# Attention with a mixture of experts: the softmax reciprocal moved to the product with V, that product issued earlier, one step more of depth, and the first weight split on GpSimd

## The chip, the core and the metric

The kernel runs on one core of a Trainium2 chip. Its engines work through instruction lists of their own, in order: PE (TensorE, matrix products and transposes), DVE (VectorE), ACT (ScalarE), POOL (GpSimd) and SP (SyncE, which here issues DMAs). They meet by semaphores. The metric is the device time of one execution in microseconds (us), the median over runs. Before the change it is 853.65 us (three runs, 851.12 to 854.62).

## What is computed

```python
# 4 batches, 8 heads, 512 local + 32 global tokens, head size 64
out_g = softmax(q_g @ k_all.T / 8) @ v_all                 # global rows see all 544 keys
s_l   = concat([q_l @ k_g.T / 8, where(|i - j| <= 32, q_l @ k_l.T / 8, -1e9)])
out_l = softmax(s_l) @ concat([v_g, v_l])                  # local rows: a window, and the globals
# softmax(s) = exp(s - max) / (sum + 1e-9)
x = tokens of out_g, out_l                                 # 2304 tokens of 512
e = argmax(x @ w_gate);  x = gate * sigmoid(x @ w_output_gate)[e] * (relu(x @ w1[e]) @ w2[e])
h = x @ w_in;  out = (P(h) / (Q(h) + 1e-6)) @ w_out        # P cubic, Q quadratic in |h|
```

## The kernel before

The program has three stages: attention (to about 168 us), eight experts, and the last two products. The change lies in the first, and in the first expert's weights, which are prepared during it.

Attention works through 72 units. A local unit ("l") holds 128 query rows of a pair of heads against a window of 160 keys; there are 64, four to a pair of heads. A global unit ("g") holds the global rows of four heads against all 544 keys; there are 8. Each unit passes through stages, and a loop over steps `s` (line 430) issues at each step one stage of several units, so that units are in flight together:

- `s0`: PE multiplies Q and K into the PSUM tile `sc` (L258; L287 for a global unit). DVE adds the mask and takes the row maximum (L263, one instruction for each of two heads).
- `s1`, one step later: ACT takes the exponential and the row sums (L301).
- `s2`, two steps later: POOL adds the two column blocks of `ex` that stand for the global keys (L312) and adds 1e-9 to the sums (L320, tile `r`, or `rg` for a global unit). Then, behind a `yield`, DVE takes the reciprocal (L322).
- `s3`, `KT` = 4 steps later: PE transposes `ex` (L331), DVE copies it out of PSUM as `pts`, ACT in one unit of four (L333).
- `s4`, `KV` = 5 steps later: PE multiplies by V (L358; L369 for a global unit) into the PSUM tile `xv`. After every second local unit DVE multiplies both by the reciprocals into `xrow` (L361). The next product into `xv` waits for that. For a global unit ACT scales (L373).
- `s5`, `KX` = 7 steps later: PE transposes `xrow` (L399), and ACT copies it (L400).

Within a step the order of issue is the first part of `s2`, `s3`, the reciprocal of `s2`, two background calls, `s0`, a background call, `s1`, another, `s4`, `s5`, a last background call, and then loads. The loop makes 81 steps; the last nine or so only empty the pipeline. `step_bg()` advances background work by one `yield`: the routing of the batch just done (`gate`, a chain of small DVE instructions with some products on PE, L489 to L619), and, after the third batch, `ahead`. This gathers, scales and transposes the first expert's rows in three blocks: "g" is an indirect DMA of POOL (L780), "x" a scaling on DVE (L794), "p" four transposes on PE with their copies (L805, L785, L786). The table `AH` gives the background calls to let pass before each of these nine actions.

From step 25, in one step of four, one of 16 pieces of the first expert's weights is split into a rounded part `hi` and a rest `lo` (`W0`, `split_piece`, mode `SM0` = "act_pool"): ACT casts `hi` (L691), POOL subtracts (L695). What is left goes behind the loop.

Loads are issued by SP three pairs of heads ahead, into four buffers of each kind. After the loop the first expert's product starts (L898), and the routing of the last batch is woven into it.

Of the kernel before, what the change touches and what calls it, by code (L numbers as in the profile page):

```python
# [7 lines left out]
F32 = mybir.dt.float32  # L8
# [5 lines left out]
AF = mybir.ActivationFunctionType  # L14
ALU = mybir.AluOpType
# [13 lines left out]


WN = 15
SLAST, GW, GS, SPL, AH = 1, 3, 2, 8, (0, 0, 14, 1, 2, 0, 2, 24, 2)
NW = 0
XG = lambda nc, h: nc.vector.tensor_copy
OY = 0
# [51 lines left out]
CH = (4, 3, 4, 3, 3)  # L87
ER = {"ab": 1, "q": 2, "u": 2, "r0": 1}
CQ = lambda nc: nc.sync
SM0 = "act_pool"  # L90
KT, KV, KX = 4, 5, 7
LL = 2
OA = lambda nc, i: nc.vector
SB_ = 2
# [8 lines left out]
class Build:  # L103
# [94 lines left out]
    def attention(self, ap):  # L198
        nc, tc, t = self.nc, self.tc, self.t
        with ExitStack() as st:  # L200
# [3 lines left out]
            sp, gp, vp, lp = P("sp", 3), P("gp", 1), P("vp", 2), P("lp", 4)  # L204
# [20 lines left out]
            def load_pair(g):  # L225
                if g < B * NP:
                    load_qk(g)
                    load_v(g)

            def load_b(b):  # L230
                if b >= B:
                    return
                qg[b] = vp.tile([128, NP, 64], F32, tag="qg", name="qg")
                nc.sync.dma_start(out=qg[b], in_=t["qg"][b])
# [8 lines left out]
            st_, rs = {}, {}  # L243
# [50 lines left out]
            def s1(u):  # L294
                k = units[u]
                src, mx = st_[u]
                ssum = sp.tile([128, 2], F32, tag="ssum", name="ssum")
                if k[0] == "l":
                    ex = sp.tile([128, 2, 160], F32, tag="ex", name="ex", bufs=KT)
                    for h in range(2):  # L300
                        nc.scalar.activation(ex[:, h], src[:, h], AF.Exp, bias=mx[:, h:h + 1], scale=-1.0,  # L301
                                             accum_out=ssum[:, h:h + 1])
                else:
                    ex = gp.tile([128, S], F32, tag="exg", name="exg")
                    nc.scalar.activation(ex, src, AF.Exp, bias=mx[:, 0:1], scale=0.125, accum_out=ssum[:, 0:1])
                st_[u] = ex, ssum

            def s2(u):
                k = units[u]
                ex, ssum = st_[u]  # L310
                if k[0] == "l":
                    nc.gpsimd.tensor_tensor(out=ex[:, :, 0:32], in0=ex[:, :, 0:32], in1=ex[:, :, 128:160], op=ALU.add)  # L312
                    if k[3] % 2 == 0:
                        self.r = sp.tile([128, 2, 2], F32, tag="r", name="r")
                    r = self.r[:, k[3] % 2]
                    rs[k[1:3] + (k[3] // 2,)] = self.r
                else:
                    r = rs[u] = sp.tile([128, 1], F32, tag="rg", name="rg", bufs=1)
                    ssum = ssum[:, 0:1]
                nc.gpsimd.tensor_scalar(out=r, in0=ssum, scalar1=1e-9, scalar2=None, op0=ALU.add)  # L320
                yield
                nc.vector.reciprocal(out=r, in_=r)  # L322
                st_[u] = ex

            def s3(u):
                k = units[u]
                pr = st_[u]
                pt = ps_t.tile([128, 4, 128], F32, tag="pt", name="pt")
                if k[0] == "l":
                    for h in range(2):  # L330
                        nc.tensor.transpose(pt[:, h, :], pr[:, h, 0:128], self.ident)  # L331
                    pts = sp.tile([128, 2, 128], F32, tag="pts", name="pts", bufs=KV - KT + 1)
                    (nc.scalar.copy if k[3] in PA else nc.vector.tensor_copy)(pts, pt[:, 0:2])  # L333
                else:
                    pt2 = ps_t.tile([128, 4, 128], F32, tag="pt", name="pt")
                    pts = gp.tile([128, 7, 128], F32, tag="ptg", name="ptg")
                    for c, (at, rows, _) in enumerate(GCH):
                        nc.tensor.transpose((pt, pt2)[c // 4][:rows, c % 4], pr[:, at:at + rows], self.ident)
                    nc.vector.tensor_copy(pts[:, 3], pt[:, 3])
                    nc.vector.tensor_copy(pts[:96, 0:3], pt[:96, 0:3])  # L340
                    nc.scalar.copy(pts[:32, 5:7], pt2[:32, 1:3])
                    nc.scalar.copy(pts[:64, 4], pt2[:64, 0])
                st_[u] = pts

            def s4(u):
                k = units[u]
                pts = st_.pop(u)
                if k[0] == "l":
                    _, b, p, i = k
                    g = b * NP + p  # L350
                    if i % 2 == 0 and p == 0:
                        xrow[b, i // 2] = xp.tile([128, 2, DM], F32, tag="xrow", name="xrow")
                    if i % 2 == 0:
                        self.xv = next(halves)
                    xps = self.xv.rearrange("p (i h d) -> p i h d", i=2, h=2)
                    for h in range(2):
                        for j in range(4):
                            nc.tensor.matmul(xps[32 * j:32 * j + 32, i % 2, h], lhsT=pts[:, h, 32 * j:32 * j + 32],  # L358
                                             rhs=vw[g][:, 4 * i + j, 64 * h:64 * h + 64], start=True, stop=True)
                    if i % 2 == 1:  # L360
                        nc.vector.tensor_tensor(  # L361
                            out=xrow[b, i // 2][:, :, 128 * p:128 * p + 128].rearrange("p i (h d) -> p i h d", h=2), in0=xps,
                            in1=rs.pop((b, p, i // 2)).unsqueeze(3).to_broadcast([128, 2, 2, 64]), op=ALU.mult)
                else:
                    _, b, q = k
                    xps = next(halves)[:, 0:64]
                    for c, (_, rows, n) in enumerate(GCH):
                        for a in range(4):
                            nc.tensor.matmul(xps[32 * a:32 * a + 32], lhsT=pts[:rows, c, 32 * a:32 * a + 32],  # L369
                                             rhs=vw[b * NP + 2 * q + a // 2][:rows, n, 64 * (a % 2):64 * (a % 2) + 64],  # L370
                                             start=(c == 0), stop=(c == len(GCH) - 1))
                    xr = gp.tile([128, 64], F32, tag="xr", name="xr", bufs=2)
                    nc.scalar.activation(xr, xps, AF.Copy, scale=rs.pop(u))  # L373
                    nc.sync.dma_start(
                        out=self.xbuf[S * b:S * b + SG, 256 * q:256 * q + 256].rearrange(
                            "t (a d) -> a t d", a=4), in_=xr)
                    st_[u] = xr
# [44 lines left out]
            n = len(units)  # L422
            w0 = self.split_set(0, SM0)
            when, at = {}, {u[1:]: k for k, u in enumerate(units)}
# [3 lines left out]
                    k = min(k, at[B - 1, 1, 0])  # L428
                when.setdefault(k, []).append(g)
            for s in range(n + KX + LL):  # L430
                norm = s2(s - 2) if 0 <= s - 2 < n else iter(())
                next(norm, None)
                if 0 <= s - KT < n:
                    s3(s - KT)
                next(norm, None)
                for _ in range(NB):
                    self.step_bg()
                if s < n:
                    s0(s)
                self.step_bg()  # L440
                if 0 <= s - 1 < n:
                    s1(s - 1)
                self.step_bg()
                if 0 <= s - KV < n:
                    s4(s - KV)
                if 0 <= s - KX < n:
                    s5(s - KX)
                self.step_bg()
                for g in when.get(s, ()):
                    load_pair(g)  # L450
                    if g % NP == 0:
                        load_b(g // NP)
                if s in RS:
                    self.load_raw(0, RS.index(s))
                while pend and pend[0][0] <= s:
                    i = pend.pop(0)[1]
                    if i == 0:
                        self.lfin = ps_s.tile([128, 2, 512], F32, tag="sc", name="lfin")
                        self.lgs = self.gt.tile([128, 512], F32, tag="lgs", name="lgs", bufs=1)
                    o = self.lfin[:, 0, 256 * i:256 * i + 256]  # L460
                    self.logits(o, xT[B - 1, i])
                    nc.scalar.copy(self.lgs[:, 256 * i:256 * i + 256], o)
                if W0(s):
                    next(w0, None)
# [945 lines left out]
```

## Time and profile before

| | us |
|---|---|
| median of three runs (lowest, highest) | 853.65 (851.12, 854.62) |
| the profiled execution | 850.67 |
| its span, first to last instruction | 849.1 |
| PE, DVE, ACT, POOL busy in the span | 788.6, 602.1, 542.9, 355.0 |
| mean granted TensorE clock | 0.974 |

The rows below come from this one profiled execution, and times in it count from the start of its span. Busy time of PE is the union of its matrix instructions, whose ends are modelled. "PEld" is the loading of weights into PE, which overlaps. "PEclk" is the share of full clock that was granted. In the views of waits, "A <- B" says that an instruction of A was held last by B; "issue" is time in which the engine waited for nothing that the profile shows. A name before `<-` in an instruction is its output, the names behind are inputs.

### The profile page before, as it was taken

What the parts mean: (1) busy time and instruction counts of PE and PEld (TensorE: products, weight loads), DVE (VectorE), ACT (ScalarE), POOL (GpSimd) and SP (SyncE); (2) the same over time, 40 slices, a digit from 0 to 9 for tenths busy, and PEclk for the clock granted to TensorE, in tenths of its full rate; (3) what the DMA queues carried; (4) which work ended last, traced back from release to release, by engine and by line L of the source; (5) the groups of instructions that cost most, each with busy time, mean ns of one, the idle gap of its engine ahead of it and who ended that gap; (6) DMA issues with size and microseconds to landing.
All of it is one profiled execution on the core that took longest, in us unless ns stands there. A gap on an engine that the chain in (4) does not pass through costs nothing. (4 is left out here: it accounts for less than half of the span.)

```text
span 849.1 us, 17307 instructions
## 1 busy us (share of the span) xinstructions
PE 788.6 (93%) x6261; PEld 663.8 (78%) x6262; DVE 602.1 (71%) x1385; ACT 542.9 (64%) x1205; POOL 355.0 (42%) x419
## 2 busy tenths in 40 slices
PE   8998888688799999999997999999999999999995
PEld 4665555487697999999795788888878889888883
DVE  4766577485273987876186999868878886788784
ACT  4765664543463666665256888767777775777774
POOL 2333333445161666563062677542243324233332
PEclk9998999988899999999999999999999999999999
DMA  9796662356273888988144432011010001000100
GB/s 354 238 354 240 247 225 84 93 169 187 72 238 135 263 318 286 331 290 280 53 168 126 132 97 91 1 50 37 14 38 13 13 1 38 13 2 0 38 1 37
DMA packets 50702, 113.91 MB, mean 134 GB/s; under 512 B 8707, under 2 KB 22292, under 8 KB 48554
## 3 DMA queue, kind: packets, MB, share of 16 engines
q1 hardware_dynamic: 41946, 98.23, 34.4%
q0 software_dynamic: 4288, 10.06, 3.5%
q10 hardware_dynamic: 4368, 4.34, 1.5%
q8 instruction: 56, 0.92, 0.4%
q14 instruction: 44, 0.36, 0.2%
HBM read 96.99 MB, written 19.56 MB: 137 GB/s over the span
## 5 line engine op out<-in xcount | busy, mean ns | idle before, releaser
L1185 POOL TENSOR_TENSOR q<-q,ab 128x384 f32<-128x384 f32 (+1 forms) x80 | 101.8, 1273 | 203.1 <-ACT q L1184 194.9
L1221 PE MATMUL acc<-slot,gh 128*128 128x512 f32 x544 | 171.1, 395 | 3.7 <-ACT gh L1193 1.9
L695 POOL TENSOR_TENSOR slot<-raw,slot 128x512 fp32r<-128x512 f32 x80 | 110.0, 1379 | 104.1 <-ACT slot L691 100.7
L1114 PE MATMUL ph<-x2c,slot 128*128 128x512 f32 (+1 forms) x576 | 132.5, 379 | 5.6 <-DVE u L1187 3.9
L1114 PEld LDWEIGHTS ph<-x2c,slot 128*128 128x128 f32 x576 | 106.5, 189 | 26.4 <-DVE u L1187 5.1
L1221 PEld LDWEIGHTS acc<-slot,gh 128*128 128x128 f32 x544 | 101.1, 187 | 25.7 <-ACT gh L1193 2.8
L1221 PE MATMUL acc<-slot,gl 128*128 128x512 f32 x272 | 107.6, 396 | 0.3 <-DVE gl L1194 0.3
L910 PE MATMUL acc<-hT,slot 128*128 128x256 f32 (+1 forms) x768 | 105.2, 288 | 0.2 <-DVE hT L904 0.2
L910 PEld LDWEIGHTS acc<-hT,slot 128*128 128x128 f32 x768 | 98.0, 191 | 0.5 <-DVE hT L904 0.4
L691 ACT CAST slot<-raw 128x512 fp32r<-128x512 f32 x144 | 84.9, 618 | 9.3 <-DVE yt L916 5.9
L1196 ACT ACTIVATE r<-q,cab 128x384 f32<-128x384 f32 (+1 forms) x80 | 52.8, 660 | 45.7 <-POOL q L1185 45.5
L1202 DVE SCALAR_TENSOR_TENSOR q<-q,r 128x384 f32<-128x384 f32 (+1 forms) x64 | 38.0, 593 | 52.0 <-ACT r L1198 51.9
L1114 PE MATMUL ph<-xa,slot 128*128 128x384 f32 x384 | 72.0, 336 | 1.5 <-DVE u L1209 1.5
L1193 ACT CAST gh<-u 128x384 fp32r<-128x384 f32 (+1 forms) x80 | 44.6, 558 | 42.1 <-DVE u L1209 35.2
L1114 PEld LDWEIGHTS ph<-xa,slot 128*128 128x128 f32 x384 | 67.7, 188 | 4.6 <-DVE u L1209 1.9
L695 DVE TENSOR_TENSOR slot<-raw,slot 128x512 fp32r<-128x512 f32 x64 | 60.4, 946 | 13.3 <-ACT slot L691 12.5
L301 ACT ACTIVATE ex<-sm,mx 128x160 f32<-128x160 f32 x128 | 53.6, 421 | 13.1 <-DVE mx L263 11.7
L1221 PEld LDWEIGHTS acc<-slot,gl 128*128 128x128 f32 x272 | 50.9, 187 | 13.4 <-DVE gl L1194 1.0
L1184 ACT ACTIVATE q<-ab,cab 128x384 f32<-128x384 f32 (+1 forms) x80 | 59.8, 747 | 0.0
L1183 ACT ACTIVATE u<-ph,cab 128x384 f32<-128x384 f32 (+1 forms) x80 | 56.7, 709 | 0.0
L1187 DVE SCALAR_TENSOR_TENSOR u<-u,cab,ph 128x384 f32<-128x384 f32 (+1 forms) x80 | 53.4, 668 | 2.8
L898 PE MATMUL ph<-xa,slot 128*128 128x256 f32 x384 | 53.8, 293 | 1.2 <-ACTq L996 1.2
(212 smaller groups left out, 1466.5 us busy)
## 6 DMA issues: line engine op xcount, KB each, us to landing
raw<-in_w_dram SPq DMA_DIRECT2D x76, 512.0 KB, 6.7
vw<-in_vw_dram SPq DMA_DIRECT2D x16, 1024.0 KB, 9.7
r<-in_w_dram SPq DMA_DIRECT2D x20, 512.0 KB, 5.6
kw<-in_kw_dram SPq DMA_DIRECT2D x16, 384.0 KB
raw<-wf SPq DMA_DIRECT2D x10, 512.0 KB, 4.8
xg<-ybuf SPq DMA_DIRECT2D x17, 256.0 KB, 4.4
qt<-in_qT_dram SPq DMA_DIRECT2D x16, 256.0 KB, 4.8
xbuf<-xrow SPq DMA_DIRECT2D x8, 512.0 KB
```

The costliest lines, as they stand in the source:

```text
L301: nc.scalar.activation(ex[:, h], src[:, h], AF.Exp, bias=mx[:, h:h + 1], scale=-1.0, accum_out=ssum[:, h:h + 1])
L691: nc.scalar.copy(hi, r)
L695: eng.tensor_tensor(out=lo[:, c], in0=r[:, c], in1=hi[:, c].bitcast(F32), op=ALU.subtract)
L898: nc.tensor.matmul(ph, lhsT=W[:, b, 2 * k + s // 4, c:c + 128], rhs=x[:, a, k, :n], start=(i == 0), stop=(i == 11))
L910: nc.tensor.matmul(acc[m][:, :n], lhsT=W[:, b, 8 + f, 128 * m:128 * m + 128], rhs=hT[f % nh][:, a, :n], start=(f == 0 and i == 0), stop=(f ...
L1114: self.nc.tensor.matmul(ph[:, :w], lhsT=l[a], rhs=r[b], start=(k == 0 and i == 0), stop=(k == 3 and i == 2))
L1183: nc.scalar.activation(u, h, AF.Identity, scale=a3, bias=a2)
L1184: nc.scalar.activation(q, ab, AF.Identity, scale=b1, bias=b0)
L1185: nc.gpsimd.tensor_tensor(out=q, in0=q, in1=ab, op=ALU.mult)
L1187: nc.vector.scalar_tensor_tensor(out=u, in0=u, scalar=a1, in1=h, op0=ALU.add, op1=ALU.mult)
L1196: nc.scalar.activation(r0, q, AF.Ln, bias=eps1)
L1221: nc.tensor.matmul(accs[i], lhsT=l[a], rhs=Wo[:, b, f, :], start=(f == 0 and j == 0), stop=(f == 15 and j == 2))
```

## The change

- `s2` no longer takes the reciprocal. `s4` does: for a local unit once for two units, on all four sums of a row, just ahead of the second product with V; for a global unit just ahead of ACT's scaling.
- `s4` is issued right behind `s3` and ahead of the scores of `s0`. `KT`, `KV` and `KX` grow by one to 5, 6 and 8, so the loop has 82 steps. `r` gets four buffers, `rg` two.
- `SM0` = "pool": POOL makes `hi` itself with a copy, and then subtracts (`split_piece`, unchanged). ACT has no part in the 16 pieces.
- `AH` changes: the nine delays are 3, 5, 11, 3, 5, 0, 5, 20, 2 calls, before 0, 0, 14, 1, 2, 0, 2, 24, 2.

```diff
-SLAST, GW, GS, SPL, AH = 1, 3, 2, 8, (0, 0, 14, 1, 2, 0, 2, 24, 2)
+SLAST, GW, GS, SPL, AH = 1, 3, 2, 8, (3, 5, 11, 3, 5, 0, 5, 20, 2)
...
-SM0 = "act_pool"
-KT, KV, KX = 4, 5, 7
+SM0 = "pool"
+KT, KV, KX = 5, 6, 8
...
             def s2(u):
...
                     if k[3] % 2 == 0:
-                        self.r = sp.tile([128, 2, 2], F32, tag="r", name="r")
+                        self.r = sp.tile([128, 2, 2], F32, tag="r", name="r", bufs=4)
...
                 nc.gpsimd.tensor_scalar(out=r, in0=ssum, scalar1=1e-9, scalar2=None, op0=ALU.add)
-                yield
-                nc.vector.reciprocal(out=r, in_=r)
                 st_[u] = ex
...
             def s4(u):
...
+                    if i % 2 == 1:
+                        r = rs.pop((b, p, i // 2))
+                        nc.vector.reciprocal(out=r, in_=r)
                     for h in range(2):
                         for j in range(4):
                             nc.tensor.matmul(xps[32 * j:32 * j + 32, i % 2, h], lhsT=pts[:, h, 32 * j:32 * j + 32],
...
-                    nc.scalar.activation(xr, xps, AF.Copy, scale=rs.pop(u))
+                    r = rs.pop(u)
+                    nc.vector.reciprocal(out=r, in_=r)
+                    nc.scalar.activation(xr, xps, AF.Copy, scale=r)
...
             for s in range(n + KX + LL):
-                norm = s2(s - 2) if 0 <= s - 2 < n else iter(())
-                next(norm, None)
+                if 0 <= s - 2 < n:
+                    s2(s - 2)
                 if 0 <= s - KT < n:
                     s3(s - KT)
-                next(norm, None)
+                if 0 <= s - KV < n:
+                    s4(s - KV)
                 for _ in range(NB):
                     self.step_bg()
                 if s < n:
                     s0(s)
...
-                if 0 <= s - KV < n:
-                    s4(s - KV)
```

On DVE, two neighbouring steps early in attention, where no background work stands between, read before (`ISA` is the mask step with its read of the maximum):

```order
L322 RECIPROCAL r<-r 128x2
L263 ISA sm,mx<-sc,mask 128x160
L263 ISA mx 128x1
L263 ISA sm,mx<-sc,mask 128x160
L263 ISA mx 128x1
L333 COPY pts<-pt 128x256
L322 RECIPROCAL r<-r 128x2
L263 ISA sm,mx<-sc,mask 128x160
L263 ISA mx 128x1
L263 ISA sm,mx<-sc,mask 128x160
L263 ISA mx 128x1
L361 TENSOR_TENSOR xrow<-xv,r 128x2x128
```

And with the change (line numbers shift by two or so):

```order
L331 COPY pts<-pt 128x256
L263 ISA sm,mx<-sc,mask 128x160
L263 ISA mx 128x1
L263 ISA sm,mx<-sc,mask 128x160
L263 ISA mx 128x1
L331 COPY pts<-pt 128x256
L356 RECIPROCAL r<-r 128x4
L362 TENSOR_TENSOR xrow<-xv,r 128x2x128
L263 ISA sm,mx<-sc,mask 128x160
L263 ISA mx 128x1
L263 ISA sm,mx<-sc,mask 128x160
L263 ISA mx 128x1
```

One reciprocal for a pair of units stands where two stood, and the multiplication into `xrow` has moved from behind the mask steps of its step to ahead of them.

On POOL, around the first weight piece (`slot_81` is the first expert's weight buffer), the list reads before:

```order
L312 TENSOR_TENSOR ex<-ex 128x2x32
L320 TENSOR_SCALAR r<-ssum 128x2
L695 TENSOR_TENSOR slot_81<-raw_74,slot_81 128x512
L312 TENSOR_TENSOR ex<-ex 128x2x32
L320 TENSOR_SCALAR r<-ssum 128x2
```

And with the change:

```order
L312 TENSOR_TENSOR ex<-ex 128x2x32
L320 TENSOR_SCALAR r<-ssum 128x2
L690 CAST slot_81<-raw_74 128x512
L691 TENSOR_TENSOR slot_81<-raw_74,slot_81 128x512
L312 TENSOR_TENSOR ex<-ex 128x2x32
L320 TENSOR_SCALAR r<-ssum 128x2
```

The cast has come into POOL's list, ahead of the subtraction; the sums of the next unit stand behind both, as they stood behind the one.

On PE, from the last scores but one on (`xg_90`, `xg_91` are gathered rows of the first expert), before:

```order
L331 MATMUL pt<-ident,ex 128x128 x2
L258 MATMUL sc<-kw,qt 64x160 x4
L358 MATMUL xv<-vw,pts 32x64 x8
L385 MATMUL pt<-ident,xr 64x128
L331 MATMUL pt<-ident,ex 128x128 x2
L258 MATMUL sc<-kw,qt 64x160 x4
L805 MATMUL pt<-ident,xg_90 128x128 x4
L358 MATMUL xv<-vw,pts 32x64 x8
L805 MATMUL pt<-ident,xg_91 128x128 x4
L331 MATMUL pt<-ident,ex 128x128 x2
```

And with the change, from the last scores on:

```order
L258 MATMUL sc<-kw,qt 64x160 x4
L388 MATMUL pt<-ident,xr 64x128
L329 MATMUL pt<-ident,ex 128x128 x2
L359 MATMUL xv<-vw,pts 32x64 x8
L329 MATMUL pt<-ident,ex 128x128 x2
L359 MATMUL xv<-vw,pts 32x64 x8
L491 MATMUL pt<-xTg,cst 32x128 x4
L402 MATMUL pt<-ident,xrow 128x128 x2
L329 MATMUL pt<-ident,ex 128x128 x2
L359 MATMUL xv<-vw,pts 32x64 x8
L484 MATMUL pt<-ident,xrow 128x128
L807 MATMUL pt<-ident,xg_90 128x128 x4
```

The transposes of the first gathered block stood right behind the last scores; now three transposes of `ex` and three products with V stand between.

## Rows read from the trace of the kernel before

**Rows 1.** Busy us by stretch: PE, PEld, DVE, ACT, POOL; then PEclk, DMA share, GB/s
```profile
24.00:64.00 40.00, 38.94 (x783) 26.65 (x784) 28.77 (x151) 27.41 (x111) 13.45 (x44) 1.00 0.90 314
...
64.00:144.00 80.00, 66.54 (x1206) 44.57 (x1205) 52.08 (x289) 45.65 (x177) 28.02 (x73) 0.91 0.61 209
...
144.00:168.00 24.00, 16.92 (x310) 10.17 (x307) 12.28 (x55) 12.48 (x45) 10.24 (x18) 0.93 0.23 72
```

**Rows 2.** The same stretches, score products alone (L258): PE, PEld
```profile
24.00:64.00 40.00, 9.93 (x160) 4.03 (x160) 1.00 0.90 314
...
64.00:144.00 80.00, 15.47 (x232) 6.34 (x232) 0.91 0.61 209
```

**Rows 3.** The same view, weight casts on ACT alone (L691)
```profile
64.00:144.00 80.00, 5.52 (x9) 0.91 0.61 209
```

**Rows 4.** Waits of PE, 64 to 144: us in total, times, longest
```profile
PE xv L358 <- DVE xrow L361: 5.6, 7, 1.8
...
PE xv L369 <- DVE xrow L361: 1.4, 2, 1.2
...
PE pt L331 <- DVE r L322: 1.4, 2, 0.7
...
PE pt L331 <- DVE pts L333: 1.1, 1, 1.1
```

**Rows 5.** Waits of DVE, same stretch
```profile
DVE r L322 <- POOL r L320: 12.3, 8, 2.0
```

**Rows 6.** Timeline, one weight piece: start, us, engine, line, shapes, [idle before]
```profile
84.64 0.61 ACT L691 CAST slot<-raw 128x512 fp32r<-128x512 f32 x1
...
85.32 1.27 POOL L695 TENSOR_TENSOR slot<-raw,slot 128x512 fp32r<-128x512 f32 x1 [2.71 <-ACT slot L691]
...
86.66 0.22 POOL L320 TENSOR_SCALAR rg<-ssum 128x1 f32<-128x1 f32 x1
...
86.92 0.16 DVE L322 RECIPROCAL rg<-rg 128x1 f32<-128x1 f32 x1 [1.46 <-POOL rg L320]
...
88.01 0.43 PE L358 MATMUL xv<-vw,pts 128*32 128x64 f32 x16 [1.20 <-DVE xrow L361]
```

**Rows 7.** Groups of PE instructions, 64 to 144, of the gate: busy us, mean ns
```profile
L615 PE MATMUL ta<-ob,oa 128*128 128x136 f16 x11 | 2.2, 252 | 0.0
...
L489 PE MATMUL lgT<-xT,cst 128*32 128x256 f32 x32 | 2.1, 385 | 0.0
...
L514 PE MATMUL lg<-ident,lgs 128*128 128x128 f32 x8 | 1.3, 287 | 0.3 <-ACT lgs L509 0.3
```

**Rows 8.** Timeline, DVE instructions beside long POOL instructions
```profile
138.91 0.31 DVE L604 TENSOR_SCALAR ob<-iota,slf,cst 128x136 f16<-128x136 f16 x1
...
140.84 1.39 DVE L604 TENSOR_SCALAR ob<-iota,slf,cst 128x136 f16<-128x136 f16 x1
...
140.92 1.26 POOL L695 TENSOR_TENSOR slot<-raw,slot 128x512 fp32r<-128x512 f32 x1 [1.37 <-PE sc L258]
...
169.92 2.13 DVE L521 COPY L<-Lg 128x16 f32<-128x16 f32 x1
```

**Rows 9.** Groups of POOL copies, whole span: busy us, mean ns
```profile
L161 POOL CAST tri<-cst 128x256 bf16<-128x256 f32 x1 | 0.4, 393 | 0.0
...
L155 POOL COPY run_cnt<-cst 128x8 f32<-128x8 f32 x1 | 0.2, 194 | 0.1
```

**Rows 10.** Group of DVE mask steps, 8 to 168
```profile
L263 DVE CUSTOM_DVE_ANT_0 sm<-sc,mask 128x160 f32<-128x160 f32 x124 | 34.9, 319 | 5.9 <-PE sc L258 3.8 <-ACT ex L301 0.8 <-PE pt L331 0.3
```

**Rows 11.** Timeline of PE, one undisturbed step
```profile
31.65 0.38 PE L331 MATMUL pt<-ident,ex 128*128 128x128 f32 x2
...
32.39 0.43 PE L358 MATMUL xv<-vw,pts 128*32 128x64 f32 x16
```

**Rows 12.** Timeline behind the last scores
```profile
153.66 0.17 DVE L322 RECIPROCAL r<-r 128x2 f32<-128x2 f32 x1 [2.20 <-POOL r L320]
...
155.66 1.01 PE L805 MATMUL pt<-ident,xg 128*128 128x128 f32 x4 [3.00 <-issue]
```

More of the change, by code (lines that the diff above doesn't have):

```diff
@@ L317, in s2 @@
                 else:
-                    r = rs[u] = sp.tile([128, 1], F32, tag="rg", name="rg", bufs=1)
+                    r = rs[u] = sp.tile([128, 1], F32, tag="rg", name="rg", bufs=2)
                     ssum = ssum[:, 0:1]
                 nc.gpsimd.tensor_scalar(out=r, in0=ssum, scalar1=1e-9, scalar2=None, op0=ALU.add)
-                yield
-                nc.vector.reciprocal(out=r, in_=r)
                 st_[u] = ex
@@ L362, in s4 @@
                             out=xrow[b, i // 2][:, :, 128 * p:128 * p + 128].rearrange("p i (h d) -> p i h d", h=2), in0=xps,
-                            in1=rs.pop((b, p, i // 2)).unsqueeze(3).to_broadcast([128, 2, 2, 64]), op=ALU.mult)
+                            in1=r.unsqueeze(3).to_broadcast([128, 2, 2, 64]), op=ALU.mult)
                 else:
```

## The prediction

> **What bounds the kernel now.** I read the busy time by stretch first, to see where PE, the busiest engine, stands idle. From 24 to 64 us it is busy for 38.94 of 40 us at full clock; from 64 to 144 for 66.54 of 80, at a mean granted clock of 0.91 [rows 1]. The reader is to see a stage in two halves that do the same work at two speeds. Counting that work comes next. A local unit issues eight records of L258, so the first stretch makes 160/8 = 20 local units, 2.0 us each, and the second 232/8 = 29, 2.76 us each [rows 2]. Global units are spread evenly among them. What differs is that the weight pieces have begun: nine casts in the second stretch [rows 3].
>
> Third came the waits. PE's largest are for the multiplication into `xrow` (5.6 and 1.4 us), for the reciprocal (1.4) and for a copy behind it (1.1) [rows 4], all work of DVE. DVE's largest wait in turn is the reciprocal's, for POOL: 12.3 us in eight times [rows 5]; nine pieces, eight long waits. Last I followed one piece through the timeline: ACT casts at 84.64, POOL subtracts from 85.32 to 86.59, so the sum of a unit comes out only at 86.66 to 86.88. The reciprocal has stood 1.46 us at the head of DVE's queue, with the mask steps and `xrow` behind it, and PE has waited 1.20 us for `xrow` when it goes on at 88.01 [rows 6]. So POOL is idle most of the time (28.02 of 80 us busy [rows 1]), and yet its order bounds the stage: a long instruction of POOL stands ahead of a short one on which DVE waits within the same step.
>
> **The reciprocal and the order of issue.** The change takes that wait away: the reciprocal stands four steps behind the sum it reads, 4 x 2.0 = 8 us. POOL's other product, the added columns, is read by PE's transposes three steps later, 6 us, against one piece of some 2 us.
>
> What is it worth? At the pace of the first stretch, the 29 units take 58.0 us; the gate's products, mostly absent there, add 2.2 + 2.1 + 1.3 = 5.6 [rows 7], together 63.6. The ceiling is 80 - 63.6 = 16.4 us, and it holds PE's idle time as well as what the lower clock costs. Of the idle 80 - 66.54 = 13.46 us, the four waits of [rows 4] are 9.5, or 71%; the others belong to other causes and stay. 0.71 x 16.4 = 11.6 us. The clock I take along with the waits, since it stands at 1.00 where PE does not stall and at 0.91 where it does [rows 1]: of its two levels, 1.2 and 2.4 GHz, a mean of 0.91 means 18% of the time at the lower.
>
> There are 32 + 8 reciprocals for 64 + 8, and at 0.16 us [rows 6] DVE saves 32 x 0.16 = 5.1 us. I count nothing: DVE is busy 52.08 of 80 us [rows 1], so the time it saves lies beside PE; 5.1 is the other end.
>
> What is late next? `xrow` now stands ahead of the mask steps and waits for the product, which PE issues right behind the transposes; DVE's copy of `pts` covers nearly all of it. In the eight global units ACT's scaling waits for the product and has two exponentials behind it that stood ahead. Uncovered, that is at most a step each, 8 x 2.0 = 16 us; the exponentials are transposed four steps (8 us) later, so I take nothing. On SP the store of the global rows falls one step behind against the loads, which run three pairs, 12 units or 24 us, ahead: nothing. V's buffers come free later by about one pair of transposes; the same cover.
>
> **The split on POOL.** ACT loses 16 casts of 0.61 us [rows 6]. It is busy 45.65 of 80 [rows 1] and no wait of PE in [rows 4] names it: nothing. POOL gains 16 copies that the trace does not have. From below: 393 ns for 256 columns and 194 for 8 give 0.80 ns a column [rows 9], hence 0.194 + 504 x 0.0008 = 0.60 us. From above: the two-input subtraction of the same tile, 1.27 us [rows 6]. I take 0.60, for a one-input cast is what the nearest row shows; the range keeps 1.27. A piece then holds POOL for 0.60 + 1.27 = 1.87 us (2.54 at most), in about 7.5 us, and the queue behind it has the three steps of cover named above. The Trainium skill, "GPSIMD Engine Reference", section 3.1, gives 769 ns for 512 elements of a one-input loop; by it a piece would be 2.04 us, and the sum the same.
>
> The copies do have a price on DVE. Of the gate's instructions one of L604 took 1.39 us in place of 0.31: it began at 140.84 and ended at 142.23, as POOL's subtraction ended (140.92 + 1.26 = 142.18) [rows 8]. One hit in nine pieces cost 1.1 us. A window longer by 1.87/1.27 is hit more often and holds longer, by 1.47 each, so 1.1 becomes 2.4, 1.3 more. Every piece in full would be 9 x 1.87 = 16.8. I take 2.5, near the row, raised because copy, subtraction and the sums behind them will now run without a gap.
>
> **Depth, delays and the tail.** One step more of depth is one more step to empty: a transposition and a product, 0.38 + 0.43 = 0.8 us [rows 11]. Against it, PE stood 3.00 us at 152.66 before the first gathered block, whose transposes stood right behind the last scores; DVE had come late to its scaling after a reciprocal that waited 2.20 us for POOL [rows 12]. That wait goes, and the block stands three products later. The other end is that the wait moves to the third block, whose gather follows the first block's transposes more closely: up to the same 3.0 back. I take 3.0 - 0.8 = 2.2 gained, and keep -0.8 for the range. The buffers cost nothing. What follows attention (routing of the last batch, gathers, first expert) hangs on its end and shifts with it.
>
> **Sum.** 11.6 - 2.5 + 2.2 = 11.3 us. The profiled span of 849.1 becomes 837.8; with the 850.67 - 849.1 = 1.57 us around it, 839.4. The profiled execution lay 853.65 - 850.67 = 2.98 below the median, so the median to expect is 842.4, say 842. At the good end (whole ceiling, whole gap, no price on DVE: 16.4 + 3.0 - 0.8 = 18.6) it is 835; the forecast's own range is 835 to 848.
>
> **Rivals.**
>
> *Slower: the pieces block DVE.* The mechanism is that of [rows 8], its place the three gates and the tail, its price up to 1.87 us a piece. Before it, the gain is 11.6 + 2.2 = 13.8. Over 16 pieces it decides from 13.8/16 = 0.86 us a piece, and the kernel is slower by more than 0.5% from (13.8 + 4.3)/16 = 1.13. With 13 pieces in full, 24.3 us, the time is 853.65 - 13.8 + 24.3 = 864. For it: a copy of 16 columns took 2.13 us [rows 8]. Against it: the 124 mask steps average 319 ns with a dozen pieces beside them [rows 10], so most of DVE's work is not touched. Chance 7%. The Trainium skill speaks against the change here: "SBUF — State Buffer", section "Who interferes with whom", says that GpSimd and VectorE share a port pair as an exclusive lock, which a VectorE instruction needs if it has two inputs in SBUF or runs in a two-port mode, and that the later one blocks fully. The L604 that ended with POOL's instruction agrees; by the rule alone any such instruction that meets a piece pays in full.
>
> *No change: new waits for the old.* DVE stays in order behind PE, the gates bring its small instructions in bunches, and half of the 11.6 comes back as waits of PE for `pts` and `xrow`; the tail's wait moves to the third block. Then 5.8 - 2.5 - 0.8 = 2.5 us are gained: 851. For it: PE also waits for ACT and for the gate, 13.46 - 9.5 = 4 us that stay. Against it: from 24 to 64 us the same DVE work with the same order leaves PE 1.06 us idle [rows 1]. Chance 15%.
>
> *The gain is given back later.* If the transfers behind attention set the pace of the first experts, half remains: 853.65 - 5.6 = 848. Against it: the DMA share is 0.23 at the end of attention, and inside it 0.61, which at 68 us for 80 becomes 0.72, under the 0.90 that the first stretch bears [rows 1]. Chance 5%.
>
> **Chances.** The forecast has 73%. About 0.5%, 4.3 us, is what a measurement of this kernel can tell from no change. The forecast and the third rival lie beyond it: faster 78%; same 15%; slower 7%. The range of 835 to 851 leaves out the slower rival, half of the second, and the forecast's edges.
>
> **What would show it.** In the profile after: no reciprocal of `r` waits for POOL, where 12.3 us stood. From 64 us to the end of attention, a local unit takes 2.2 to 2.4 us, and the granted clock is above 0.95. POOL's copy takes 0.6 to 0.8 us. `xrow` no longer leads PE's waits. The first expert's product starts some 11 us before 168. I am wrong if L604, L600 and their like average far over their 0.3 us (the first rival), if PE waits as long for `pts` or `xrow` as before (the second), or if attention ends 11 us sooner and the span does not (the third).

## The result, and the profile after

The changed kernel took 845.62 us (median of four runs), the kernel before 854.13 beside it. The ratio is 0.9898 [0.9852, 0.9945]. A repeat in five rounds gave 843.77 (842.38 to 844.53) against 852.72, 0.9897 [0.9865, 0.9929]: some 8.8 us faster. One of the first four executions, the profiled one, took 1492.84 us for a reason that no run here shows; the ratio leaves it out, and the profile shown here is of the repeat.

First the busy time by stretch of the profiled execution of the repeat (842.38 us, span 840.8), columns as in [rows 1]:

```profile
24.00:64.00 40.00, 38.12 (x796) 25.55 (x796) 25.88 (x133) 26.52 (x111) 13.83 (x43) 1.00 0.77 254
64.00:144.00 80.00, 72.42 (x1410) 48.04 (x1407) 62.78 (x312) 45.69 (x190) 36.88 (x94) 0.98 0.70 240
144.00:168.00 24.00, 17.44 (x232) 12.39 (x229) 10.64 (x37) 8.93 (x31) 15.47 (x23) 0.86 0.46 138
```

PE's idle time in the middle stretch fell from 13.46 to 7.58 us. The score products alone, the same kernel, answer to [rows 2]:

```profile
64.00:144.00 80.00, 17.57 (x272) 7.26 (x272) 0.98 0.70 240
```

272 records are 34 local units in 80 us, 2.35 us each, where there were 29 at 2.76. The same two rows of a second profiled execution of the changed kernel (847.41 us):

```profile
64.00:144.00 80.00, 74.10 (x1364) 48.35 (x1361) 61.07 (x304) 45.36 (x186) 35.71 (x88) 0.89 0.67 225
...
64.00:144.00 80.00, 18.47 (x267) 7.45 (x264) 0.89 0.67 225
```

It does nearly as much at a granted clock of 0.89, PE being busy longer and idle less. So neither PE's idle time nor its clock gives the pace by itself. The waits of PE from 64 to 144 us, first execution, against [rows 4]:

```profile
PE pt L402 <- ACT ptg L340: 2.5, 2, 1.8
PE xv L359 <- ACT xr L376: 1.1, 2, 0.6
PE pr L551 <- DVE ohb L542: 1.0, 1, 1.0
```

No `xrow` and no `r` among them. Two of the three stood in the kernel before as well, though [rows 4] does not show them:

```profile
PE pt L399 <- ACT ptg L342: 1.7, 1, 1.7
PE pr L549 <- DVE ohb L540: 1.6, 1, 1.6
```

Only the wait for ACT's scaling of a global unit (`xr`) is new, and it is small. DVE's waits, against [rows 5]:

```profile
DVE sm L263 <- PE sc L258: 6.2, 8, 2.1
DVE mx L289 <- PE scg L287: 5.0, 4, 1.6
DVE pts L331 <- PE pt L329: 1.0, 2, 0.7
```

DVE waits for the products it needs next, no longer for POOL. POOL's, the same stretch:

```profile
POOL ex L312 <- ACT ex L301: 23.7, 21, 3.3
POOL rg L320 <- ACT exg L305: 10.6, 5, 4.7
```

POOL waits for the softmax, and for no cast. One piece of weights in the timeline, against [rows 6]:

```profile
82.80 0.61 POOL L690 CAST slot<-raw 128x512 fp32r<-128x512 f32 x1
...
83.50 1.27 POOL L691 TENSOR_TENSOR slot<-raw,slot 128x512 fp32r<-128x512 f32 x1
...
84.52 0.17 DVE L356 RECIPROCAL r<-r 128x4 f32<-128x4 f32 x1
84.79 0.42 DVE L362 TENSOR_TENSOR xrow<-xv,r 128x256 f32<-128x256 f32 x1
...
85.28 0.22 POOL L320 TENSOR_SCALAR rg<-ssum 128x1 f32<-128x1 f32 x1 [0.51 <-ACT exg L305]
```

Cast and subtraction run back to back without a bracket, a reciprocal of older sums starts while POOL is still in the subtraction, and `xrow` follows at once. POOL needs 1.97 us from the cast's start to the subtraction's end, where the pair ACT and POOL took 1.95, but POOL stood 2.71 us more for the cast before.

The cost of the split, by groups of instructions over attention (us, mean ns):

```profile
L602 DVE TENSOR_SCALAR oa<-iota,slf 128x128 f16<-128x128 f16 x12 | 3.8, 314 | 0.0
L606 DVE TENSOR_SCALAR ob<-iota,slf,cst 128x136 f16<-128x136 f16 x12 | 3.7, 308 | 0.0
L533 DVE TENSOR_TENSOR df<-L,m 128x32 f32<-128x32 f32 x3 | 1.8, 604 | 0.1
L356 DVE RECIPROCAL r<-r 128x4 f32<-128x4 f32 x32 | 5.3, 166 | 0.0
...
L690 POOL CAST slot<-raw 128x512 fp32r<-128x512 f32 x16 | 9.8, 611 | 0.8
```

The first three are of the gate; in the kernel before, from 8 to 168 us, they read

```profile
L600 DVE TENSOR_SCALAR oa<-iota,slf 128x128 f16<-128x128 f16 x12 | 3.1, 256 | 0.0
L604 DVE TENSOR_SCALAR ob<-iota,slf,cst 128x136 f16<-128x136 f16 x12 | 4.8, 402 | 0.0
L531 DVE TENSOR_TENSOR df<-L,m 128x32 f32<-128x32 f32 x3 | 0.7, 232 | 0.0
```

The cast takes 611 ns. Most of the gate's instructions stay near their length; the long ones have moved, from L604 to L533.

To see where the time went, the whole way to the first expert was cut at two marks that stand in every kernel: the 33rd of the 128 mask steps (L263), ahead of the first weight piece, and the last score product (L258). In the changed kernel:

```profile
40.05 0.31 DVE L263 CUSTOM_DVE_ANT_0 sm<-sc,mask 128x160 f32<-128x160 f32 x1
...
146.90 0.50 PE L258 MATMUL sc<-kw,qt 64*64 64x160 f32 x8
```

and in the kernel before:

```profile
36.02 0.33 DVE L263 CUSTOM_DVE_ANT_0 sm<-sc,mask 128x160 f32<-128x160 f32 x1
...
152.16 0.50 PE L258 MATMUL sc<-kw,qt 64*64 64x160 f32 x8
```

The tail is counted from these scores to the first expert's product (`ph<-slot`, at 163.47 and 168.01); the rest is what remains of the span from there. All profiled executions but the one of 1492.84 us, in us, the clock being that of 144 to 168 us (the last column counts the waits for `r`; one of 1.5 us for `rg` stands besides in the three kernels with 8.0 or more):

```
kernel            to the  33rd to      tail  its    rest   DVE waits for
                  33rd    last scores        clock         POOL's sums, 64:144
before            36.0    116.1        15.9  0.93   681.1  12.3 (8 times)
before, again     36.6    115.3        18.0  0.71   677.2  12.2 (8)
changed           40.1    106.9        16.6  0.86   677.3  none
changed, again    37.3    108.7        18.7  0.65   681.2  none
split alone       38.0    107.2        14.2  1.00   679.3  0.6 (2)
no split          36.5    109.2        17.5  0.72   682.3  none
reciprocal alone  39.3    106.8        16.1  0.72   677.9  none
cast ahead        36.7    109.0        18.6  0.58   677.7  0.9 (3)
pieces doubled    36.5    117.5        20.1  0.71   682.6  8.0 (7)
reciprocal+split  37.7    108.1        13.4  1.00   678.4  none
gathers first     37.3    107.4        16.3  0.79   677.3  none
old delays        37.4    105.4        16.1  0.86   679.9  none
old depth         38.1    105.4        15.2  0.79   677.3  none
```

The second column of times is the one to read: 115.3 to 117.5 us with the wait, 105.4 to 109.2 without it, and nothing between. In the means of two executions each, the changed kernel gains 115.74 - 107.76 = 8.0 us there, loses 38.66 - 36.31 = 2.4 ahead of it and 17.6 - 16.9 = 0.7 in the tail.

### The profile page after: what moved, and what is told of

The parts are those of the page before. It is cut to its first block, busy times and chain, and to the rows that moved or that the text cites. A ratio compares the mean times of both kernels' runs of the same rounds, so it can differ in the third digit from the quotient of the medians.

```text
span 1491.2 us, 17290 instructions
## 1 busy us (share of the span) xinstructions
PE 1466.2 (98%) x6261; PEld 1092.5 (73%) x6262; DVE 607.4 (41%) x1353; ACT 535.9 (36%) x1189; POOL 352.7 (24%) x435
## 4 chain that ended last, share of the span: by engine, by line
PE 50%; issue 0%; POOL 0%; POOLq 0%; ACT 0%
PE acc L1223 25%; PE ph L1116 25%; POOL out_dram L1240 0%; POOLq L1407 0%; ACT raw L1238 0%; POOL ix L1234 0%; PE acc L1284 0%; POOLq L1240 0%
## 5 line engine op out<-in xcount | busy, mean ns | idle before, releaser
L1223 PE MATMUL acc<-slot,gh 128*128 128x512 f32 x544 | 309.9, 672 | 0.0
L1116 PE MATMUL ph<-x2c,slot 128*128 128x512 f32 (+1 forms) x576 | 256.3, 637 | 1.7 <-ACTq L998 1.3
L1116 PEld LDWEIGHTS ph<-x2c,slot 128*128 128x128 f32 x576 | 171.4, 299 | 80.5 <-issue 71.2
L1223 PEld LDWEIGHTS acc<-slot,gh 128*128 128x128 f32 x544 | 161.8, 298 | 81.9 <-issue 74.6
L912 PE MATMUL acc<-hT,slot 128*128 128x256 f32 (+1 forms) x768 | 196.5, 442 | 0.0
L912 PEld LDWEIGHTS acc<-hT,slot 128*128 128x128 f32 x768 | 187.2, 336 | 0.7
L1223 PE MATMUL acc<-slot,gl 128*128 128x512 f32 x272 | 183.4, 674 | 0.0
L1116 PE MATMUL ph<-xa,slot 128*128 128x384 f32 x384 | 140.6, 557 | 0.0
L1116 PEld LDWEIGHTS ph<-xa,slot 128*128 128x128 f32 x384 | 114.7, 301 | 26.6 <-issue 20.0
L900 PEld LDWEIGHTS ph<-xa,slot 128*128 128x128 f32 x384 | 93.1, 350 | 2.0 <-ACTq L998 1.6
L900 PE MATMUL ph<-x2c,slot 128*128 128x256 f32 x288 | 73.3, 448 | 1.8 <-ACTq L998 1.1
L900 PEld LDWEIGHTS ph<-x2c,slot 128*128 128x128 f32 x288 | 69.7, 353 | 3.1 <-ACTq L998 1.7
```

The lines of the kernel that those rows point to most:

```text
L900: nc.tensor.matmul(ph, lhsT=W[:, b, 2 * k + s // 4, c:c + 128], rhs=x[:, a, k, :n], start=(i == 0), stop=(i == 11))
L912: nc.tensor.matmul(acc[m][:, :n], lhsT=W[:, b, 8 + f, 128 * m:128 * m + 128], rhs=hT[f % nh][:, a, :n], start=(f == 0 and i == 0), stop=(f ...
L1116: self.nc.tensor.matmul(ph[:, :w], lhsT=l[a], rhs=r[b], start=(k == 0 and i == 0), stop=(k == 3 and i == 2))
L1223: nc.tensor.matmul(accs[i], lhsT=l[a], rhs=Wo[:, b, f, :], start=(f == 0 and j == 0), stop=(f == 15 and j == 2))
```

## The experiments

The theory after the result: the reciprocal's wait went, with it the pace of the pieces' stretch rose, and the tail gave nothing. The rivals: the gain is the relief of ACT; it is the order, depth and delays; the split costs DVE what the rest gained. All ratios are to the kernel before on the same chip.

**The changed kernel again**, nothing edited, in five rounds.

> The changed kernel once more, for an undisturbed profile and a tighter ratio. Expected by the prediction: 843 to 847 us, ratio about 0.990. No reciprocal of r waits for POOL between 64 us and the end of attention (12.3 us before), a local unit takes 2.2 to 2.4 us there (2.76 before), POOL's copy of a weight piece takes 0.6 to 0.8 us, the first expert's product starts 8 to 11 us before 168. If instead the new waits took the place of the old, PE's waits for xrow and pts there stay near 9 us; if pieces block DVE, L600 and L604 average far over 0.3 us.

0.9897 [0.9865, 0.9929], shown above. This execution granted PE a clock of 0.72 in its first 24 us and reached the 33rd mask step at 40.1 us; the other one had 0.93 there and 37.3. So 2.8 us of the late start belong to the execution; whether the rest (37.3 for 36.0 and 36.6 before) belongs to the change is open.

**The split alone**, on the kernel before:

```diff
-SM0 = "act_pool"
+SM0 = "pool"
```

> The kernel before with one edit: the weight split is on POOL alone (SM0 = pool). Theory A (the cost is the reciprocal, which waits in the same step for a sum that stands behind a piece on POOL): a piece holds POOL for some 1.9 us in place of 1.27, the wait of the reciprocal stays or grows by up to 0.6 us a piece, 0 to 9 us slower, ratio 1.000 to 1.010. Theory B (what gains is that POOL no longer waits for ACT's cast, and ACT has 10 us less to do): most of the gain is here, ratio 0.990 to 0.995.

0.9908 [0.9872, 0.9944], as much as the whole change. The reciprocal still stands in the step of its sum, behind pieces that now hold POOL for two instructions in place of one. Yet DVE's wait for it is

```profile
DVE r L322 <- POOL r L320: 0.6, 2, 0.3
```

for 12.3 before. So it was not the length of POOL's instruction. What went is a wait of POOL itself. In the kernel before, 64 to 144 us, POOL's waits read

```profile
POOL slot L695 <- ACT slot L691: 23.2, 8, 4.9
```

Eight long waits, as many as DVE's: POOL stood in order at the subtraction until ACT had reached the cast, and the sums stood behind it.

**The change without the split**:

```diff
-SM0 = "pool"
+SM0 = "act_pool"
```

> The changed kernel with one edit undone: the weight split is on ACT and POOL again (SM0 = act_pool). Theory A: nothing on DVE waits for the sums any more, so the time stays within 0.4% of the changed kernel, ratio to the kernel before 0.988 to 0.994. Theory B: the gain goes, ratio 0.996 to 1.000.

0.9863 [0.9823, 0.9903]. That is a little better than the 0.988 to 0.994 of theory A, and theory B is out. POOL waits for ACT's cast as before, and nobody minds, since the reciprocal reads sums four steps old:

```profile
POOL slot L697 <- ACT slot L693: 21.7, 9, 3.8
```

**The reciprocal alone**, on the kernel before; order, depth, delays and split stay:

```diff
             def s2(u):
-                yield
-                nc.vector.reciprocal(out=r, in_=r)
...
             def s4(u):
+                    if i % 2 == 1:
+                        r = rs.pop((b, p, i // 2))
+                        nc.vector.reciprocal(out=r, in_=r)
```

and the same for a global unit, with four buffers of `r` and two of `rg`.

> The kernel before with the reciprocal alone moved to the step of the product with V (and the buffers of r and rg that it needs); order of issue, depth, split and delays as before. Theory A: the wait of 12.3 us of the reciprocal for POOL goes and with it most of the gain, ratio 0.990 to 0.994. Theory C (the gain comes from issuing V's product and xrow ahead of the scores, and from the depth): most of the gain is missing here, ratio 0.996 to 1.000, with the transposes of PE waiting for POOL's added columns in place of DVE's reciprocal.

0.9841 [0.9798, 0.9885], by the median the better half, and more than the 0.990 to 0.994 expected. So either remedy brings the whole gain; whether they add is asked further down (reciprocal and split).

**ACT's cast one piece ahead**, on the kernel before: the cast of piece q + 1 is issued before POOL's subtraction of piece q; nothing else moves.

```diff
+            cast(0)
             for q in range(16):
+                if q < 15:
+                    cast(q + 1)
                 nc.gpsimd.tensor_tensor(out=self.slot[0][:, 1, q, :], in0=raw(q),
                                         in1=self.slot[0][:, 0, q, :].bitcast(F32), op=ALU.subtract)
```

> The kernel before; ACT's cast of a weight piece is issued one piece (four steps) ahead of POOL's subtraction, all else as before. Splitting alone had gained as much as the whole change, so theory A' is: what held the sums, and the reciprocal behind them, was POOL standing at a subtraction whose cast ACT had not reached (23.2 us in eight times between 64 and 144 us), not the length of its instructions. A' expects the 12.3 us of the reciprocal's wait to fall under 4 and a ratio of 0.988 to 0.993. Theory L (the 1.27 us of the subtraction itself stand in front of the sums) expects the wait to stay over 8 us and a ratio of 0.997 to 1.002.

0.9856 [0.9806, 0.9905]. ACT still does all 16 casts, POOL all 16 subtractions, the reciprocal stands where it stood, and the wait is

```profile
DVE r L322 <- POOL r L320: 0.9, 3, 0.3
```

From 64 to 144 us no wait of POOL for a cast is left. That shows the late cast as the cause: not ACT's load, which is the same, but the moment at which POOL meets the subtraction. Nor does the gain need the halved number of reciprocals: here and with the split alone all 72 stand.

**The pieces doubled**: the split alone, each copy and subtraction of the first expert made twice.

```diff
+            for _ in range(2 if e == 0 else 1):
-            nc.gpsimd.tensor_copy(hi, r)
+                nc.gpsimd.tensor_copy(hi, r)
```

> The kernel before with the split on POOL alone, and every copy and subtraction of the first expert's weights made twice, so that a piece holds POOL for about 3.8 us in place of 1.9, without waiting for ACT. Theory L: the reciprocal waits some 1.9 us more for each of the nine pieces between 64 and 144 us, 10 us and more in all, and the time is that of the kernel before or above, ratio 1.000 to 1.010. Theory A': most of the length is covered as long as POOL comes to the piece early; the wait grows by 2 to 5 us over that of the single split, ratio 0.992 to 0.998.

1.0059 [1.0025, 1.0093]. The wait is back without any wait for ACT:

```profile
DVE r L322 <- POOL r L320: 8.0, 7, 2.4
```

So length does count, from some size on: with a piece of 0.61 + 1.27 = 1.9 us the wait is 0.6 us, and one of 3.8 us costs 117.5 - 107.2 = 10 us more between the marks. The time is that of theory L; theory A' had the wait grow by only 2 to 5 us, and missed. DVE is not slowed much by the longer pieces: the gate's 87 instructions on it (from 30 to 154 us, in the 24 forms that all kernels share, each form's number times its mean) take 23.8 us, and 22.8 with the split alone.

**Reciprocal and split**, the old order, depth and delays (the edits of the second and the fourth experiment together).

> The kernel before with the reciprocal moved to the product with V and the split on POOL alone; order of issue, depth and delays as before. Each edit alone gave 0.984 and 0.991. If both remove the same wait, they don't add: ratio 0.983 to 0.991. If they remove different costs, 0.975 to 0.980.

0.9821 [0.9774, 0.9869], the lowest ratio of all, 838.19 us. If the two added, it would be 0.9841 x 0.9908 = 0.975. That lies just below the interval, but has one of its own (some 0.006 either way, from the two) which overlaps, and 0.9821 lies between the two ranges expected: the ratios do not decide. From the 33rd mask step to the last scores the kernel takes 108.1 us, against 106.8 and 107.2 of the two edits apart: no addition there. PE's waits here:

```profile
PE xv L359 <- DVE xrow L362: 5.3, 6, 2.3
PE xv L370 <- DVE xrow L362: 3.8, 3, 2.1
```

PE waits 9.1 us for `xrow`, more than the 5.6 + 1.4 of [rows 4], in a kernel that is faster by 1.8% (idle in all it is 80 - 69.82 = 10.2 us, for 13.5). The wait of PE for `xrow` was the face of the trouble and not its measure.

**The gathers first**, on the changed kernel: the first two gathers are issued some background calls sooner, and the first scaling is held back by as many.

```diff
-AH = (3, 5, 11, 3, 5, 0, 5, 20, 2)
+AH = (0, 0, 19, 3, 5, 0, 5, 20, 2)
```

> The changed kernel with the first two gathers issued without delay and the scaling of the first block held back by as much (delays 0, 0, 19, 3, 5, 0, 5, 20, 2). In the changed kernel DVE stood 1.95 us for the second gathered block at 152.16, and PE 2.58 us behind it; last scores to first product of the first expert took 16.3 us, 15.6 before. Theory G (the second gather was issued too late, 4.4 us before its scaling): that wait goes, last scores to first product take 13.5 to 14.5 us, ratio to the kernel before 0.985 to 0.988. Theory H (the tail is bound by the chain of transposes, copies and products): the wait goes but the tail stays at 15 us or more, ratio 0.988 to 0.991.

0.9892 [0.9837, 0.9946], and the tail is 16.3 us for 16.6 and 18.7. The second scaling no longer waits for its gather (below, in the part on the tail); it begins at 148.78 without a bracket. Yet the tail is hardly shorter than the 16.6 us of the first execution, and a single tail tells little: those of one kernel differ by 2.1 us.

**The old delays** (`AH` of before) and **the old depth** (`KT, KV, KX` = 4, 5, 7), each on the changed kernel.

> The changed kernel with the nine delays of the first expert's gathers, scalings and transposes as before. From the last scores to the first expert's product took 15.6 us before, 16.4 with the change, and 13.9 and 13.2 with the split on POOL in the old order and with the old delays. If the delays make the difference, it takes 13 to 14.5 us here and the ratio is 0.983 to 0.988; if order and depth make it, 16 to 17 us and 0.988 to 0.991.

> The changed kernel with the depth of before (KT, KV, KX = 4, 5, 7), the product with V still issued ahead of the scores. If the step of depth costs what the prediction gave it, 0.8 us at the end, and buys nothing that the moved reciprocal has not bought, the time is that of the changed kernel within 0.3%, ratio 0.987 to 0.991, last scores to first product 15 to 16 us. If the depth covers POOL's pieces, PE's transposes now wait for the added columns, over 3 us between 64 and 144 us, and the ratio is 0.992 to 0.996.

0.989 [0.982, 0.9959] and 0.9861 [0.9817, 0.9905]. Neither part of the change buys anything that these runs can tell; at the old depth PE has no wait for POOL's added columns from 64 to 144 us, so the pieces do not need the extra step. On one chip and in the same rounds the changed kernel took 843.77 us, without the split 841.60, with the reciprocal alone 841.11.

**One more execution** of each of the two kernels, for the scatter of single executions.

> The kernel before once more, for a second profile. What the change is said to remove must be there again: DVE's reciprocals wait 10 to 14 us for POOL between 64 and 144 us, and 56 to 60 score units' records (224 to 240) are issued there. Whether the first 24 us (clock 0.93, 84 records) and the first expert (41.9 us to its remainder) are the same is open: if they vary by some us, differences there between single profiles say nothing of the change.

> The changed kernel once more, for a second undisturbed profile. Between 64 and 144 us no reciprocal waits for POOL and 270 to 280 score records are issued, as in the first. If the low clock from 11 to 24 us of the first profile (mean 0.72 over 24 us, 64 records) belongs to the change, it comes again; if it is a matter of the single run, the clock is 0.85 or more and the last scores come at 143 to 146 us in place of 147.1.

848.66 and 847.41 us. Of what was expected, the waits came as said (12.2 us and none) and the score records nearly (240, and 267 for 270 to 280). The means of the two profiled pairs differ by 849.67 - 844.90 = 4.8 us where the timed medians differ by nearly 9: the profiled executions lie below the median for the kernel before (850.67 and 848.66 against 852.72), and on both sides of it for the changed one (842.38 and 847.41 against 843.77). The table says where much of it sits: the start, 2.4 us later, at which kernels with the code of before up to that point (before, split alone, cast ahead, pieces doubled) stand at anything from 36.0 to 38.0, and the others at 36.5 to 40.1.

## Why the prediction came out right

The sign and the time came out: 842 was forecast, 843.8 and 845.6 measured, in the range of 835 to 851. The steps did so in part.

**The bound, and what goes.** Right in what stood still: DVE's reciprocal, for POOL's sums in its own step; and right in what would be seen, no such wait and a local unit of 2.35 us. Wrong in what POOL was doing. The step that failed is "a long instruction of POOL stands ahead of a short one on which DVE waits within the same step". The instruction was short enough; what stood ahead was POOL's own wait for ACT's cast. It was in the rows: in [rows 6] the subtraction at 85.32 carries "[2.71 <-ACT slot L691]", more than twice its 1.27 us, and I read past the bracket to the duration.

**The 11.6 us, less 2.5 for the port.** Net 9.1; measured 8.0 from the 33rd mask step to the last scores (from 115.3 - 108.7 = 6.6 to 116.1 - 106.9 = 9.2). The sum was made for 64 to 144 us alone; by its own measure, the local units in that stretch (29 and 30 before, 34 and 33.4 after), it is 8.1 to 11.8 us. So the sum was of the right size, its working only in part. The four waits of [rows 4] did go, yet the clock that I took along with them was 0.98 in one execution and 0.89 in the other, at nearly the same pace. The 71% was a share of PE's waits by name, and those are no measure of it, as the run with 9.1 us of waits for `xrow` shows. PE's whole idle time from 64 to 144 us does tell the kernels with the wait (13.5 to 13.9 us) from those without (5.9 to 10.2), but not how fast these are: the two at 5.9 and 10.2 take 108.7 and 108.1 us between the marks. Nor is DVE's wait the price: from 36 to 152 us it was 15.7 and 17.0 us before, and about half came back. One reading was off besides: the gate's products are not "mostly absent" from the first stretch, where L489 and L514 are busy for 1.1 and 0.7 us against 2.1 and 1.3 later, so the ceiling was too low by 1.8 x 29/20 = 2.6 us. The sum held, and the two weights behind it did not. That the saved reciprocals count for nothing was right: the split alone and the cast ahead save none, and gain as much. What sets the pace now was not isolated. DVE is the next busiest, 62.78 of 80 us, and its waits above are for PE's products.

**The split: "no wait of PE in [rows 4] names it: nothing."** This is the other failure. One wait of PE for ACT (1.7 us, for `ptg`) did stand in that view, outside the rows shown, and so the largest were not "all work of DVE"; but it was not this one that counted. By busy time ACT had room, and the split alone brings 0.9908: the casts mattered through the queue they stood in, not through their 9.8 us. Both halves of the change are remedies for the one wait, so a sum over its parts would have counted it twice had I priced them both.

**The copy and the port.** The copy took 611 ns, forecast 0.60. The Trainium skill, "GPSIMD Engine Reference", section 3.1, gives 769 ns for such a one-input loop; the measurement decides. L604, which was hit in [rows 8], is L606 now and averages 308 ns, L602 314: far from a piece's length, which refutes the slower rival at this size. The 2.5 us can be read from the runs: the gate's 87 instructions on DVE, counted as with the pieces doubled, take 23.6 us with the change and 20.9 without the split, 22.8 with the split alone and 20.2 before. The split costs DVE 2.6 to 2.7 us; what of it reaches the total is not shown. The Trainium skill, "SBUF — State Buffer", section "Who interferes with whom", says that of two instructions that need the shared pair the one that issues first has it and the other blocks fully. Single instructions here do pay: the gathered block's scaling took 1.08 us beside POOL's subtraction, which had begun before it (below), and 0.47 to 0.53 without one. The L604 of [rows 8] is less plain than the prediction had it: by the trace it began 0.08 us ahead of the subtraction, and was held all the same.

**The tail, +2.2.** Measured -0.7, about the other end that was named (-0.8), though the tails of one kernel differ by 2.1; the 3 us between the two are more than the 11.3 - 8.8 = 2.5 by which the whole forecast was too large. The wait moved, as that sentence said, though to the second block and not the third. The rows behind the last scores, against [rows 12]:

```profile
147.79 1.07 POOL L782 DMA_INDIRECT xg<-xbuf,ix  x1 [0.28 <-PE pt L388]
...
150.05 0.38 PE L329 MATMUL pt<-ident,ex 128*128 128x128 f32 x2
...
151.70 1.26 POOL L691 TENSOR_TENSOR slot<-raw,slot 128x512 fp32r<-128x512 f32 x1
...
152.16 1.08 DVE L796 TENSOR_SCALAR xg<-xg 128x512 f32<-128x512 f32 x1 [1.95 <-DMA xg<-xbuf,ix]
153.16 0.41 DVE L331 COPY pts<-pt 128x256 f32<-128x256 f32 x1
...
153.63 1.06 PE L807 MATMUL pt<-ident,xg 128*128 128x128 f32 x4 [2.58 <-DVE pts L331]
```

Attention now ends before the second gather lands. DVE has the scaling of that block at the head of its queue, waits 1.95 us for the landing and is then held beside POOL's subtraction; the copy of `pts` behind it, of transposes done at 150.43, begins only at 153.16, and PE, which waits for that copy, has lost 2.58 us (in the second execution the same two waits are 2.79 and 3.16). It is the pattern of the reciprocal once more: ready work behind an instruction that waits. Whether the deeper loop or the delays lengthen the tail stays open; the experiments on both lie within the scatter of the tails.

**The end of it all.** The first expert's product was to start some 11 us before 168; it started at 163.5 and 164.6, since the start was 2.4 us late and the tail 3 us longer than forecast. What follows the product takes 677.2 to 681.2 us in either kernel, so nothing was given back there.

**The rivals.** Blocked DVE: false here. New waits for old: in part, the tail's, and 1.1 us of PE's for ACT's scaling. Given back later: not seen behind the tail.

## What to carry to other kernels

When a wait is put down to an in-order engine that is mostly idle, look at what that engine was itself waiting for just then, in the bracket of the instruction ahead, before pricing its instructions. Where two edits relieve one wait, price the wait once and try each alone: here any of three (reciprocal later, cast on POOL, cast one piece earlier) brought 0.9 to 1.6%, and two together hardly more. Compare between marks that both kernels share, since start and tail of single executions scatter by 2 to 3 us here, which can hide a small gain.

## What was not expected of the hardware

The tail's length goes with the granted clock of the single execution: 13.4 and 14.2 us where it was 1.00, 17.5 to 20.1 in five of the six executions where it was 0.58 to 0.72 (16.1 in the sixth). Which of the two causes the other is open, as is whether the split with the old order, depth and delays, which the two shortest have in common, plays a part. The clock from 64 to 144 us varied from 0.89 to 0.98 in one kernel, at 267 and 272 score records. And a gather of 128 rows issued at 147.79 was read by DVE only at 152.16, 4.4 us later, 1.95 of it a wait for the landing.
